# GpSimd issues the stores out of the staging buffers from the second block on, and the pacing bound of attention is 1.25 in place of 1.15

## The chip, the cores and the metric

One core of a Trainium2 chip runs the whole program. The metric is the device time of one execution in microseconds; the median of three timed executions is quoted, and a profiled execution stands beside it.

## What is computed

Three layers follow each other. The first is attention over 4 batches of 8 heads with 576 positions of 64 values: a coarse one on keys, queries and values averaged over 4 positions, and a local one for |i - j| < 4, added up.

```
out_d = softmax(scale * q_d k_d^T) v_d        # q_d, k_d, v_d: means of 4 positions
out_up = repeat(out_d, 4, axis=2)
out_local = softmax(where(|i - j| < 4, scale * q k^T, -1e9)) v
x = (out_up + out_local) as (2304, 512)
x = (sigmoid(x @ w_gate) * (x @ w_val)) @ w_out        # 512 x 1536, 512 x 1536, 1536 x 512
h = x @ w_in                                           # 512 x 2048
out = (h * tanh(softplus(h))) @ w_out2                 # 2048 x 512
```

The inputs are float64 in memory.

## The kernel before

**Precision and staging.** A weight tile is loaded by `load64` (L173, a DMA on SyncE, SP for short) as pairs of integers, and `narrow` makes floats of it: one ScalarE instruction (L180), three on VectorE (L182, L183, L187). `split` then makes two reduced-precision parts of every operand: the high part by a ScalarE cast (L192), the low one by a subtraction (L193) on VectorE. Each product is three TensorE matmuls: high by high, high by low, low by high.

**Blocks.** The program goes batch by batch, `block(b)`, b = 0 to 3, with 576 tokens each: `m1` (L977 to L979) makes gate and value, L982 and L983 combine them, and `fin` splits the product into G; `m1out` (L1008 to L1012) multiplies by w_out. While block b runs, the attention of block b + 1 is woven in by `weave`, and in blocks 1 and 2 also the weights of the second layer's output matrix, which are narrowed, split and written back to DRAM for later ("parked", `park_o2`, L1087). Block 1 runs from about 240 to 400 us, block 2 to 545, block 3 to 660; the second layer follows.

**The staging buffers.** There are two, handed out in turn by `stage_flat`. Both the results of `m1out` (ScalarE L1022 writes the high part, VectorE L1023 the low part, then the store L1028 to x2d) and the parked halves (cast L192, subtraction L193, store L1087 to wd2) go through them. Neither can be written again until the store that reads it has landed. There are 8 x 2 parked stores of 256 KB in block 1 and again in block 2, and 24 stores of 288 KB of results in blocks 1 to 3. All leave on SP's queue, among the loads of weights (L173, L221), of values (L332) and of tokens (L327).

**Attention.** Keys and queries are transposed (L418, L422) and averaged by GpSimd (`s_pool`, L447 and L449, into kd and qd), values by GpSimd too (`s_vpool`, L434 and L436, into vd; each asks SP for the next raw values at L332). The coarse scores are L510 into banks ps_g, with maximum L520 and L521 on VectorE and exponential L525 on ScalarE (Eg). The local part has scores L658, exponentials L680, transposes L723, copies of those by ScalarE (L97, ETl), and products L763 (ps_la); L782 adds the parts (xn), and xn is split for the next block. Attention has three PSUM banks, so a third score tile needs the exponential of an earlier one.

**What sets the order.** `weave` walks a clock of estimated costs and takes the next ready step of attention, weights or parking, or else the next piece of the block; a paced step is held back while its share of the work done is ahead of the block's own share by more than the bound of L932. The framework then schedules the instructions of each engine by a timeline of its own, so a change in who issues what can reorder all engines. Second-layer loads (L1149 of parked weights, L1153 of x2d) are issued by GpSimd in block 3 and after.

Of the kernel before, what the change touches and what calls it, by code (L numbers as in the profile page):

```python
# [8 lines left out]
F32 = mybir.dt.float32  # L9
# [39 lines left out]
def attn_moe_kernel(  # L49
# [13 lines left out]
    PE, DVE, ACT, POOL, SP = nc.tensor, nc.vector, nc.scalar, nc.gpsimd, nc.sync  # L63
# [22 lines left out]
    def subs(b):  # L86

        a = 2 * TQ if b == 0 else SUB
        return slice(0, a), slice(a, S)
# [34 lines left out]
    NU1 = KF1 + 2 * (KF1 // 4)  # L124
# [11 lines left out]
    def products():  # L136
        if not G:
            first.release()
            gpool = ctx.enter_context(tc.tile_pool(name="gpool", bufs=1, side="left", reuse_waits="tile"))
            G.append(gpool.tile([128, KF1 * 2 * S], F32R, name="G"))  # L140
        return G[0].rearrange("p (f z t) -> p f z t", f=KF1, z=2)
# [15 lines left out]
    def stage_flat():  # L157
        i = stage_n[0] % 2
        stage_n[0] += 1
        a = OS + i * 2 * SUBM  # L160
        return R[:, a:a + 2 * SUBM]

    def stage(n):
        return stage_flat()[:, 0:2 * n].rearrange("p (z t) -> p z t", z=2)
# [3 lines left out]
    x2d = dram.tile([128, 2, KD, NT], F32, name="x2d")  # L168
# [22 lines left out]
    def split(src, hi, lo, eng):  # L191
        ACT.copy(out=hi, in_=src)  # L192
        return eng.tensor_tensor(out=lo, in0=src, in1=hi.bitcast(F32), op=ALU.subtract)  # L193
# [711 lines left out]
    done_at = {}  # L905
# [3 lines left out]
    def weave(slots, steps):  # L909


        slots, steps = list(slots), list(steps)
        total_s = sum(z.cost for z in slots) or 1.0
        total_e = sum(z.cost for z in steps if z.paced) or 1.0
        at_s = at_e = 0.0

        def ready(z):
            t = 0.0
            for name, lat in z.deps:
                if name not in done_at:  # L920
                    return None
                t = max(t, done_at[name] + lat)
            return max([t] + bank_at[0:z.banks])

        while slots or steps:
            pick, soonest = None, None
            for z in steps:
                t = ready(z)
                if t is None:
                    continue  # L930
                if t <= clock[0]:
                    if z.cost and z.paced and slots and at_e / total_e > (ENG["PACE"] if ("slot", 0, NU1 - 1) not in done_at else 1.15) * at_s / total_s + 0.01:  # L932
                        continue
                    pick = z
                    break
                soonest = t if soonest is None else min(soonest, t)
            if pick is None and slots:
                t = ready(slots[0])
                if t is not None and t <= clock[0]:
                    pick = slots.pop(0)  # L940
                    at_s += pick.cost
                elif t is not None:
                    soonest = t if soonest is None else min(soonest, t)
            elif pick is not None:
                steps.remove(pick)
                if pick.paced:
                    at_e += pick.cost
            if pick is None:
                assert soonest is not None
                clock[0] = soonest  # L950
                continue
            pick.fn()
            clock[0] += pick.cost
            done_at[pick.name] = clock[0]
            for _ in range(pick.banks):
                bank_at.pop(0)
                bank_at.append(clock[0] + pick.hold)
# [4 lines left out]
    def flush():  # L962
        while late:
            late.pop(0)()
# [30 lines left out]
    def m1out(b, c2, fg, j, ps):  # L995
        hi, lo = wq[b, KF1 + c2 * (KF1 // 4) + fg]
        c, sub = divmod(j, 2)
        ts = subs(b)[sub]
        n = ts.stop - ts.start
        gt = products()  # L1000
        if fg == 0:
            ps[j] = mm.tile([128, 512], F32, tag="mm", name="ps_o")
        p = ps[j]
        last_g = KF1 // 4 - 1
        for i in range(4):
            f = 4 * fg + i
            o = i * 256 + c * 128
            PE.matmul(p[:, 0:n], lhsT=hi[:, o:o + 128], rhs=gt[:, f, 0, ts],  # L1008
                      start=(f == 0), stop=False)
            PE.matmul(p[:, 0:n], lhsT=hi[:, o:o + 128], rhs=gt[:, f, 1, ts],  # L1010
                      start=False, stop=False)
            PE.matmul(p[:, 0:n], lhsT=lo[:, o:o + 128], rhs=gt[:, f, 0, ts],  # L1012
                      start=False, stop=(f == KF1 - 1))
        flush()
        if fg == last_g:
            if b == B - 1 and c2:

                a = free_at[j // 2] + j % 2 * 1024
                t = R[:, a:a + 2 * n].rearrange("p (z t) -> p z t", z=2)
            else:  # L1020
                t = stage(n)
            ACT.activation(out=t[:, 0, :], in_=p[:, 0:n], func=AF.Copy, scale=0.5)  # L1022
            DVE.scalar_tensor_tensor(  # L1023
                out=t[:, 1, :], in0=p[:, 0:n], scalar=0.5, in1=t[:, 0, :].bitcast(F32),
                op0=ALU.mult, op1=ALU.subtract,
            )
            t0 = b * S + ts.start
            SP.dma_start(out=x2d[:, :, 2 * c2 + c, t0:t0 + n], in_=t.bitcast(F32))  # L1028

    def block(b, extra):  # L1030

        slots = []
        ps = {}

        def add(name, fn, cost, deps):
            slots.append(Step(name, fn, cost, [(d, 0.0) for d in deps]))

        pairs = [(f, sub) for f in range(KF1) for sub in range(2)]
        if b == 0:
            n = 2 * NRING  # L1040
            pairs = sorted(pairs[:n], key=lambda z: z[1]) + pairs[n:]
        for f, sub in pairs:
            deps = [("wp", b, f, 1)]
            deps += [(b, "split", i) for i, (q0, n) in enumerate(tiles) if q0 < subs(b)[sub].stop]
            add(("slot", b, f) if sub else ("half", b, f), lambda f=f, sub=sub: m1(b, f, sub), 10.25 * (subs(b)[sub].stop - subs(b)[sub].start), deps)

        def freed():
            flush()
            done_at[b + 1, "free"] = clock[0]

        add(("freed", b), freed, 0.0, [])
        for c2 in range(2):
            for fg in range(KF1 // 4):
                u = KF1 + c2 * (KF1 // 4) + fg
                for j in range(4):
                    add(("slot", b, u) if j == 3 else ("quarter", b, u, j),
                        lambda c2=c2, fg=fg, j=j: m1out(b, c2, fg, j, ps), 1475.0, [("wp", b, u, 1)])
        weave(slots, extra)
        flush()
# [22 lines left out]
    def park_o2(j, d):  # L1082
        for a in range(2):
            t = stage_flat()
            sl = slice(a * 256, (a + 1) * 256)
            split(d[:, sl], t[:, 0:256], t[:, 256:512], DVE)
            SP.dma_start(  # L1087
                out=wd2[j, :, :, sl], in_=t[:, 0:512].rearrange("p (z f) -> p z f", z=2).bitcast(F32)
            )

    if True:
# [3 lines left out]
        for z, offs in enumerate(((0, 3), (3, 3), (3, 0))):  # L1095
            for half, off in enumerate(offs):
                mv = mask[64 * half:64 * half + 64, z, :]
                POOL.affine_select(
                    out=mv, in_=mv, pattern=[[1, WK]], compare_op=ALU.is_ge, fill=-1e9 / scale,
# [3 lines left out]
                    out=mv, in_=mv, pattern=[[-1, WK]], compare_op=ALU.is_ge, fill=-1e9 / scale,  # L1103
# [4 lines left out]
        for b in range(B - 1):  # L1108
            extra = weights(b)
            if b == 0:  # L1110
                extra = attention(0) + extra
            extra += attention(b + 1)
            if b:
                srcs = [
                    (w2_out[j * 128:(j + 1) * 128, :].rearrange("(j p) f -> p j f", p=128), 1)
                    for j in range((b - 1) * per, b * per)
                ]
                extra += narrow_steps(
                    ("o2", b), srcs, clock[0] + 1000.0,
                    lambda i, d, b=b: park_o2((b - 1) * per + i, d), 9500.0,  # L1120
                )
            block(b, extra)
# [102 lines left out]
        for t in range(NT2):  # L1225
            if t > 0:
                po = [ops.tile([128, DM], F32, tag="o", name="po") for _ in range(2)]
            for gi in range(NG):
# [6 lines left out]
                n = 4 if t else 1  # L1235
# [50 lines left out]
```

## Time and profile before

| | us |
|---|---|
| median of three executions (1067.96 to 1068.79) | 1068.76 |
| profiled execution | 1070.58 |
| its span | 1068.8 |

The granted TensorE clock of the profiled execution was 0.987 of full speed on average. In the rows below, engines are PE (TensorE), DVE (VectorE), ACT (ScalarE), POOL (GpSimd) and SP (SyncE); a time in brackets at the end of a row is the idle time of the engine before it, with what ended it. R, G, d, wd, x2d and the like are the program's tile names; R<-d at L192 and L193 is a weight split, wd<-R a parked store.

### The profile page before, as it was taken

To read this page: it belongs to the slowest core of one execution; us is meant where nothing else is said; L and a number is where in the kernel's file an instruction comes from. 1 tells how busy PE (TensorE), PEld (TensorE's weight loads), DVE (VectorE), ACT (ScalarE), POOL (GpSimd) and SP (SyncE) were. 2 spreads that over 40 slices of the span, in tenths; PEclk is the share of its full clock that TensorE was granted. 3 is DMA by queue.
4 is the path that set the end of the run, shared out by engine and by line. 5 is a ranking of instruction groups with operands and counts; after the bars stand their busy time and mean duration, and the time that the engine had idled before them with its cause. 6 is when DMAs were issued, how large, how long until landed. Compare 5 with 4: busy or idle time off the path is not lost.

```text
span 1068.8 us, 20487 instructions
## 1 busy us (share of the span) xinstructions
PE 1005.6 (94%) x8152; PEld 941.9 (88%) x8152; DVE 688.9 (64%) x1129; ACT 520.4 (49%) x1222; POOL 193.3 (18%) x235
## 2 busy tenths in 40 slices
PE   4698988899989989999999999999999999999998
PEld 3587877799979989999999999999999999999997
DVE  6966988956976448965568951867555555555552
ACT  3644656455655447564546641654443443433432
POOL 5546574640300300300000002000000000000000
PEclk9989999999989999999999999999999999999999
DMA  7638666677762358632365658212112020220001
GB/s 171 195 87 220 178 200 218 199 231 245 226 196 74 104 168 254 203 133 80 105 202 183 205 179 267 61 25 59 24 37 60 1 59 4 57 59 1 21 1 40
DMA packets 122240, 134.51 MB, mean 126 GB/s; under 512 B 54432, under 2 KB 99488, under 8 KB 122144
## 3 DMA queue, kind: packets, MB, share of 16 engines
q1 hardware_dynamic: 110336, 115.37, 35.4%
q0 software_dynamic: 11808, 17.83, 6.3%
q8 instruction: 64, 1.05, 0.4%
q14 instruction: 32, 0.26, 0.1%
HBM read 101.19 MB, written 31.98 MB: 125 GB/s over the span
## 4 chain that ended last, share of the span: by engine, by line
PE 71%; DVE 11%; DMA 8%; ACT 4%; issue 3%; POOL 2%; SPq 0%; ACTq 0%; DVEq 0%; POOLq 0%
PE h L1180 6%; PE h L1182 6%; PE h L1181 6%; PE po L1190 6%; PE po L1188 6%; PE po L1189 6%; PE ps_m L977 6%; PE ps_m L978 6%; PE ps_m L979 6%; PE ps_o L1008 4%; PE ps_o L1012 4%; PE ps_o L1010 4%; DMA araw<-in_v_dram 2%; DVE d L183 2%; DMA raw<-in_moe_w_val_dram 2%
## 5 line engine op out<-in xcount | busy, mean ns | idle before, releaser
L977 PE MATMUL ps_m<-R 128*128 128x288 f32 (+2 forms) x768 | 234.1, 308 | 4.4 <-ACT R L192 3.0
L978 PE MATMUL ps_m<-R 128*128 128x288 f32 (+2 forms) x768 | 231.5, 302 | 2.1 <-POOL R L193 2.1
L979 PE MATMUL ps_m<-R 128*128 128x288 f32 (+2 forms) x768 | 231.0, 301 | 0.5 <-POOL R L193 0.5
L977 PEld LDWEIGHTS ps_m<-R 128*128 128x128 f32 x768 | 147.6, 193 | 9.1 <-ACT R L192 3.3
L978 PEld LDWEIGHTS ps_m<-R 128*128 128x128 f32 x768 | 148.1, 193 | 2.9 <-POOL R L193 2.2
L979 PEld LDWEIGHTS ps_m<-R 128*128 128x128 f32 x768 | 148.0, 193 | 1.4 <-POOL R L193 0.9
L192 ACT CAST R<-d 128x512 fp32r<-128x512 f32 (+1 forms) x192 | 108.7, 582 | 81.0 <-DVE d L187 38.7
L193 DVE TENSOR_TENSOR R<-d,R 128x512 fp32r<-128x512 f32 (+1 forms) x158 | 105.1, 679 | 43.1 <-ACT R L192 38.4
L1008 PE MATMUL ps_o<-G,R 128*128 128x288 f32 (+2 forms) x384 | 116.6, 304 | 0.0
L1012 PE MATMUL ps_o<-G,R 128*128 128x288 f32 (+2 forms) x384 | 114.5, 298 | 0.0
L1010 PE MATMUL ps_o<-G,R 128*128 128x288 f32 (+2 forms) x384 | 114.3, 298 | 0.0
L1188 PE MATMUL po<-R,G 128*128 128x512 f32 (+1 forms) x247 | 94.5, 383 | 0.0
L1189 PE MATMUL po<-R,G 128*128 128x512 f32 (+1 forms) x247 | 94.0, 381 | 0.0
L1190 PE MATMUL po<-R,G 128*128 128x512 f32 (+1 forms) x247 | 93.5, 383 | 0.0
L1201 ACT ACTIVATE e<-e 128x1024 f32<-128x1024 f32 (+1 forms) x48 | 40.6, 846 | 107.2 <-DVE e L1200 107.2
L1182 PE MATMUL h<-R 128*128 128x256 f32 x320 | 90.2, 282 | 0.0
L1181 PE MATMUL h<-R 128*128 128x256 f32 x320 | 90.2, 282 | 0.0
L1180 PE MATMUL h<-R 128*128 128x256 f32 x320 | 90.2, 282 | 0.0
L1200 DVE TENSOR_SCALAR e<-h 128x1024 f32<-128x1024 f32 (+1 forms) x48 | 45.9, 956 | 58.2 <-PE h L1182 58.0
L1008 PEld LDWEIGHTS ps_o<-G,R 128*128 128x128 f32 x384 | 73.3, 191 | 0.8
L180 ACT ACTIVATE rebias<-raw 128x512 f32<-128x512 f32 x68 | 45.9, 675 | 56.6 <-DMA raw<-in_moe_w_out_dram 23.2
L1010 PEld LDWEIGHTS ps_o<-G,R 128*128 128x128 f32 x384 | 73.2, 191 | 0.0
(137 smaller groups left out, 2258.3 us busy)
## 6 DMA issues: line engine op xcount, KB each, us to landing
d<-wd SPq DMA_DIRECT2D x54, 512.0 KB
raw<-in_moe_w_out_dram SPq DMA_DIRECT2D x28, 512.0 KB
wd<-d SPq DMA_DIRECT2D x18, 512.0 KB
wd<-R SPq DMA_DIRECT2D x32, 256.0 KB
raw<-in_moe_w_in_dram SPq DMA_DIRECT2D x16, 512.0 KB
x2d<-R SPq DMA_DIRECT2D x24, 288.0 KB
R<-wd POOLq DMA_DIRECT2D x13, 512.0 KB, 5.7
raw<-in_moe_w_gate_dram SPq DMA_DIRECT2D x12, 512.0 KB
```

The source lines that it names most:

```text
L977: PE.matmul(p[:, 0:n], lhsT=wh, rhs=xh[:, c, ts], start=(c == 0), stop=False)
L978: PE.matmul(p[:, 0:n], lhsT=wh, rhs=xl[:, c, ts], start=False, stop=False)
L979: PE.matmul(p[:, 0:n], lhsT=wl, rhs=xh[:, c, ts], start=False, stop=(c == KD - 1))
L1008: PE.matmul(p[:, 0:n], lhsT=hi[:, o:o + 128], rhs=gt[:, f, 0, ts], start=(f == 0), stop=False)
L1010: PE.matmul(p[:, 0:n], lhsT=hi[:, o:o + 128], rhs=gt[:, f, 1, ts], start=False, stop=False)
L1012: PE.matmul(p[:, 0:n], lhsT=lo[:, o:o + 128], rhs=gt[:, f, 0, ts], start=False, stop=(f == KF1 - 1))
L1180: PE.matmul(o, lhsT=wi[:, 0, c, cs], rhs=x[:, 0, c, :], start=(c == 0), stop=False)
L1181: PE.matmul(o, lhsT=wi[:, 0, c, cs], rhs=x[:, 1, c, :], start=False, stop=False)
L1182: PE.matmul(o, lhsT=wi[:, 1, c, cs], rhs=x[:, 0, c, :], start=False, stop=(c == KD - 1))
L1188: PE.matmul(p, lhsT=g[:, 0, ts], rhs=w[:, 0, cs], start=(j == 0), stop=False)
L1189: PE.matmul(p, lhsT=g[:, 0, ts], rhs=w[:, 1, cs], start=False, stop=False)
L1190: PE.matmul(p, lhsT=g[:, 1, ts], rhs=w[:, 0, cs], start=False, stop=(j == KF2 - 1))
```

## The change

Stores of results leave on GpSimd's queue in blocks 1 to 3 (block 0 stays on SP), parked stores leave on GpSimd's queue, and the bound by which attention may be ahead of a block's own work is 1.25 from block 1 on (block 0 has ENG["PACE"] as before, which is also 1.25).

```diff
--- before.py
+++ after.py
@@ -929,7 +929,7 @@
                 if t is None:
                     continue
                 if t <= clock[0]:
-                    if z.cost and z.paced and slots and at_e / total_e > (ENG["PACE"] if ("slot", 0, NU1 - 1) not in done_at else 1.15) * at_s / total_s + 0.01:
+                    if z.cost and z.paced and slots and at_e / total_e > (ENG["PACE"] if ("slot", 0, NU1 - 1) not in done_at else 1.25) * at_s / total_s + 0.01:
                         continue
                     pick = z
                     break
@@ -1025,7 +1025,7 @@
                 op0=ALU.mult, op1=ALU.subtract,
             )
             t0 = b * S + ts.start
-            SP.dma_start(out=x2d[:, :, 2 * c2 + c, t0:t0 + n], in_=t.bitcast(F32))
+            (POOL if b else SP).dma_start(out=x2d[:, :, 2 * c2 + c, t0:t0 + n], in_=t.bitcast(F32))
 
     def block(b, extra):
 
@@ -1084,7 +1084,7 @@
             t = stage_flat()
             sl = slice(a * 256, (a + 1) * 256)
             split(d[:, sl], t[:, 0:256], t[:, 256:512], DVE)
-            SP.dma_start(
+            POOL.dma_start(
                 out=wd2[j, :, :, sl], in_=t[:, 0:512].rearrange("p (z f) -> p z f", z=2).bitcast(F32)
             )
```

On GpSimd, around the pooling of keys (kd) and queries (qd) in block 1, there stood before:

```order
L193 TENSOR_TENSOR R_77<-d_2668,R_77 128x512 x2
L447 TENSOR_TENSOR kd_3440<-kT_2894 128x576
L449 TENSOR_TENSOR kd_3440<-kd_3440,kT_2894 128x576
L447 TENSOR_TENSOR qd_3497<-qT_2938 128x576
L449 TENSOR_TENSOR kd_3440<-kd_3440,kT_2894 128x576
L449 TENSOR_TENSOR qd_3497<-qd_3497,qT_2938 128x576 x2
L434 TENSOR_TENSOR vd_4808<-araw_4802 72x128
```

and now, with the parked stores (wd2):

```order
L1087 DMA wd2_82<-R_77 256x1x256 x8
L447 TENSOR_TENSOR kd_3440<-kT_2894 128x576
L1087 DMA wd2_82<-R_77 256x1x256
L449 TENSOR_TENSOR kd_3440<-kd_3440,kT_2894 128x576
L1087 DMA wd2_82<-R_77 256x1x256
L447 TENSOR_TENSOR qd_3497<-qT_2938 128x576
L449 TENSOR_TENSOR kd_3440<-kd_3440,kT_2894 128x576
L1087 DMA wd2_82<-R_77 256x1x256
L449 TENSOR_TENSOR qd_3497<-qd_3497,qT_2938 128x576
L1087 DMA wd2_82<-R_77 256x1x256
L449 TENSOR_TENSOR qd_3497<-qd_3497,qT_2938 128x576
```

All sixteen parked stores of the block now stand ahead of, between and behind the six pooling instructions.

On TensorE, around the second pair of coarse score tiles in block 1 (ps_g_3703 and ps_g_3704; ps_m are the block's own matmuls), the difference is:

```order
 L978 MATMUL ps_m_3683<-R_77 128x288
 L979 MATMUL ps_m_3683<-R_77 128x288
-L510 MATMUL ps_g_3703<-kd_3440,qd_3497 72x144
-L510 MATMUL ps_g_3704<-kd_3440,qd_3497 72x144
-L510 MATMUL ps_g_3703<-kd_3440,qd_3497 72x144
-L510 MATMUL ps_g_3704<-kd_3440,qd_3497 72x144
+L510 MATMUL ps_g_3703<-kd_3440,qd_3497 72x144 x2
 L977 MATMUL ps_m_3728<-R_77 128x288
 L978 MATMUL ps_m_3728<-R_77 128x288
```

and 20 matmuls further on:

```order
 L977 MATMUL ps_m_3741<-R_77 128x288
 L978 MATMUL ps_m_3741<-R_77 128x288
+L510 MATMUL ps_g_3704<-kd_3440,qd_3497 72x144 x2
 L979 MATMUL ps_m_3741<-R_77 128x288
 L977 MATMUL ps_m_3741<-R_77 128x288
```

The second tile of the pair moved behind 20 of the block's matmuls. The first pair (ps_g_3620, ps_g_3621) moved 23 of them later as well:

```order
 L977 MATMUL ps_m_3648<-R_77 128x288
 L978 MATMUL ps_m_3648<-R_77 128x288
+L510 MATMUL ps_g_3620<-kd_3440,qd_3497 72x144
+L510 MATMUL ps_g_3621<-kd_3440,qd_3497 72x144
+L510 MATMUL ps_g_3620<-kd_3440,qd_3497 72x144
+L510 MATMUL ps_g_3621<-kd_3440,qd_3497 72x144
 L979 MATMUL ps_m_3648<-R_77 128x288
 L977 MATMUL ps_m_3670<-R_77 128x288
```

It stood between ps_m_3596 and ps_m_3635 before.

On ScalarE, ahead of the exponentials of the first pair (Eg_3618), there stood before:

```order
L192 CAST G_951<-sg_3609 128x288
L192 CAST R_77<-d2_4027 128x256 x2
L192 CAST R_77<-d_3668 128x512
L982 ACTIVATE sg_3661<-ps_m_3635 128x288
L525 ACTIVATE Eg_3618,sum_3617<-ps_g_3620,m_3616 72x144 x2
L525 ACTIVATE Eg_3618,sum_3617<-ps_g_3621,m_3616 72x144 x2
```

and now:

```order
L180 ACTIVATE rebias_4885<-raw_4806 128x512
L192 CAST R_77<-d2_4027 128x256 x2
L192 CAST G_951<-sg_3661 128x288
L982 ACTIVATE sg_3696<-ps_m_3670 128x288
L180 ACTIVATE rebias_5109<-raw_4974 128x512
L525 ACTIVATE Eg_3618,sum_3617<-ps_g_3620,m_3616 72x144 x2
L525 ACTIVATE Eg_3618,sum_3617<-ps_g_3621,m_3616 72x144 x2
```

The conversion of the next raw weights (L180, rebias_5109) and one more cast of G come ahead of the exponentials, and one cast of d_3668 stands earlier.

At the end of block 1 GpSimd had only its value adds (vd); now the first result stores (x2d) stand among them:

```order
L436 TENSOR_TENSOR vd_4808<-vd_4808,araw_4877 72x128
L436 TENSOR_TENSOR vd_4808<-vd_4808,araw_4942 72x128
L436 TENSOR_TENSOR vd_4808<-vd_4808,araw_4877 72x128
L1028 DMA x2d_83<-R_77 256x1x288
L436 TENSOR_TENSOR vd_4808<-vd_4808,araw_4942 72x128
L1028 DMA x2d_83<-R_77 256x1x288
L434 TENSOR_TENSOR vd_4808<-araw_5020 72x128
L436 TENSOR_TENSOR vd_4808<-vd_4808,araw_5020 72x128
```

On SP the loads of raw values (araw) and the result stores stood in turn before:

```order
L332 DMA araw_4877<-in_v_dram 72x2x256
L332 DMA araw_4942<-in_v_dram 72x2x256
L221 DMA d_4792<-wd_81 128x1024
L1028 DMA x2d_83<-R_77 256x1x288
L332 DMA araw_5020<-in_v_dram 72x2x256
L332 DMA araw_5072<-in_v_dram 72x2x256
L1028 DMA x2d_83<-R_77 256x1x288
L221 DMA d_4794<-wd_81 128x1024
L1028 DMA x2d_83<-R_77 256x1x288 x2
```

The stores left this queue. On ScalarE, the staging casts (L1022, out of ps_o) and the copies of local attention (ETl) stood there before as:

```order
L192 CAST R_77<-d_4296 128x512 x2
L1022 ACTIVATE R_77<-ps_o_4238 128x288
L1022 ACTIVATE R_77<-ps_o_4255 128x288
L97 COPY ETl_4517<-ps_lt_4512 128x512
L97 COPY ETl_4575<-ps_lt_4570 128x512
```

and now:

```order
L192 CAST R_77<-d_4296 128x512 x2
L1022 ACTIVATE R_77<-ps_o_4238 128x288
L97 COPY ETl_4517<-ps_lt_4512 128x512
L1022 ACTIVATE R_77<-ps_o_4255 128x288
L97 COPY ETl_4575<-ps_lt_4570 128x512
```

The first copy moved ahead of the fourth staging cast. At the step into block 2 ScalarE had:

```order
L192 CAST G_951<-sg_4860 128x288
L192 CAST R_77<-d2_4884 128x256
L422 COPY kT_4821<-ps_t_4822 128x4x128
L192 CAST R_77<-d2_4884 128x256
L192 CAST R_77<-xn_2864 128x4x112
L422 COPY qT_4865<-ps_t_4866 128x4x128
```

and now has:

```order
L192 CAST G_951<-sg_4860 128x288
L192 CAST R_77<-d2_4884 128x256
L422 COPY kT_4821<-ps_t_4822 128x4x128
L192 CAST R_77<-xn_2864 128x4x112
L422 COPY qT_4865<-ps_t_4866 128x4x128
L192 CAST R_77<-d2_4884 128x256
```

The cast of xn moved ahead of the second cast of d2_4884.

## Rows read from the trace of the kernel before

**Rows 1.** The page, busy time, share of the span and instructions of each engine

```profile
PE 1005.6 (94%) x8152; PEld 941.9 (88%) x8152; DVE 688.9 (64%) x1129; ACT 520.4 (49%) x1222; POOL 193.3 (18%) x235
```

**Rows 2.** Windows: us, busy time and instructions of each engine, PEclk, DMA share, GB/s

```profile
300.00:320.00 20.00, 15.83 (x103) 14.68 (x102) 14.83 (x36) 11.21 (x36) 0.00 (x0) 0.83 0.52 167
360.00:380.00 20.00, 16.01 (x170) 15.45 (x170) 9.04 (x22) 9.88 (x42) 9.19 (x18) 0.96 0.51 156
560.00:660.00 100.00, 100.00 (x758) 100.00 (x757) 65.60 (x130) 47.34 (x101) 7.35 (x13) 1.00 0.61 197
```

**Rows 3.** Waits of TensorE from 242 us on: total us, times, longest us

```profile
PE ps_g L510 <- ACT Eg L525: 5.0, 2, 4.2
PE ps_la L763 <- ACT ETl L97: 4.0, 1, 4.0
PE ps_m L977 <- ACT R L192: 3.0, 2, 2.3
PE ps_m L977 <- DVE sg L983: 1.3, 1, 1.3
PE ps_t L418 <- DVE xn L782: 0.8, 1, 0.8
```

**Rows 4.** Line L510 in 290:320 (ns min/median/max, first and last start us); TensorE's timeline (start, us)

```profile
L510 PE MATMUL ps_g<-kd,qd x24: 282/283/510, 295.5 to 317.9; 64*72 64x144 f32 x24
...
307.81 1.23 PE L510 MATMUL ps_g<-kd,qd 64*72 64x144 f32 x6 [4.17 <-ACT Eg L525]
```

**Rows 5.** Windows after the idle time at 303.6 us, columns as in group 2

```profile
309.00:313.00 4.00, 4.00 (x18) 4.00 (x18) 2.77 (x7) 2.19 (x6) 0.00 (x0) 0.50 0.77 254
314.00:318.00 4.00, 4.00 (x36) 3.79 (x34) 3.07 (x6) 2.83 (x11) 0.00 (x0) 1.00 0.01 2
```

**Rows 6.** The chain of waits through that idle time: start us, us, what

```profile
294.92 4.38 DMA wd<-R
...
299.75 0.43 DVE R L193
...
300.21 5.52 DMA wd<-R
```

**Rows 7.** ScalarE's timeline there: start us, us, instruction [idle before <-releaser]

```profile
299.63 0.43 ACT L192 CAST G<-sg 128x288 fp32r<-128x288 f32 x1
...
300.58 0.67 ACT L180 ACTIVATE rebias<-raw 128x512 f32<-128x512 f32 x1 [0.22 <-DMA raw<-in_moe_w_out_dram]
...
305.80 0.92 ACT L192 CAST R<-d 128x256 fp32r<-128x256 f32 x2 [2.74 <-DMA wd<-R]
```

**Rows 8.** Timelines of GpSimd (first row) and VectorE around the pooling

```profile
289.17 4.06 POOL L449 TENSOR_TENSOR qd<-qd,qT 128x576 f32<-128x576 f32 x2
...
289.45 2.19 DVE L193 TENSOR_TENSOR R<-d,R 128x512 fp32r<-128x512 f32 x1
...
298.86 0.68 DVE L193 TENSOR_TENSOR R<-d,R 128x512 fp32r<-128x512 f32 x1
```

**Rows 9.** SP's timeline, a parked store

```profile
293.54 0.52 SPq L1087 DMA_DIRECT2D wd<-R  x1
```

**Rows 10.** End of block 1: SP's timeline, the chain of waits (two rows), ScalarE's timeline

```profile
366.62 0.56 SPq L1028 DMA_DIRECT2D x2d<-R  x1
...
370.82 2.14 POOL vd L436 x4
...
373.34 3.44 DMA x2d<-R
...
376.88 0.41 ACT L1022 ACTIVATE R<-ps_o 128x288 fp32r<-128x288 f32 x1 [4.39 <-DMA x2d<-R]
```

**Rows 11.** GpSimd's DMA lines L1153, L1149: issue ns min/median/max; landing of L1149

```profile
L1153 POOL DMA_DIRECT2D R<-x2d x10: 740/747/936, 546.8 to 952.1; - x10
...
L1149 POOL DMA_DIRECT2D R<-wd x13: 528/536/558, 548.5 to 669.1; - x13
...
DMA to landing us min/median/max: 3.7/5.9/9.0
```

## The prediction

> **What bounds the kernel now.** I read the page's list of engines first: TensorE is busy for 94% of the span [rows 1], so a change elsewhere counts only where it moves an idle time of TensorE. The windows say where such idle time is. The change touches nothing in block 0, so I look from 242 us on: between 300 and 320 us TensorE works 15.83 of 20 us, between 360 and 380 us 16.01, while from 560 to 660 us it never stops [rows 2]. The waits of TensorE name the idle times [rows 3]: 5.0 us for a global score (L510) behind the exponential at L525, 4.0 us for L763 behind the ScalarE copy at L97, 3.0 us for L977 behind a ScalarE cast, 1.3 behind VectorE at L983 and 0.8 for L418. Together 14.1 us.
>
> I call the places A (block 1, 303.6 to 307.8 us: 4.17 of the 5.0 us) [rows 4], B (end of block 1, the 4.0 us), C (step from block 1 to 2: 0.8 us of L418 and 0.7 of L977), D (block 2: 1.3 us of L977 and the remaining 0.8 of L510) and E (block 2 to 3: the remaining 2.3 us of L977). A costs more than its idle time: from 309 to 313 us the granted clock was 0.50, the 1.2 GHz level, and 18 matmuls ran where 36 run in the 4 us from 314 on [rows 5]. That is 2.0 us. So the ceiling for any gain is 14.1 us and what the low clock adds, 2.0 us behind A and, as an upper estimate, as much behind B and E: 20 us.
>
> **A, priced.** The chain of waits through A is made of two stores out of the two staging buffers, 4.38 and 5.52 us from issue to landing [rows 6]. A parked half needs a free buffer, its cast on ScalarE waits for the store before it (305.80, 2.74 us idle) [rows 7], and L525 stands behind the casts in ScalarE's order. The store's issue on SP is no part of that wait: VectorE's subtraction ends at 299.75 + 0.43 = 300.18 us and the store is issued at 300.21 [rows 6]. So issuing from GpSimd takes nothing off this chain. It was put so late by an earlier delay: while GpSimd pools keys and queries, VectorE's two-input subtractions take 2.19 us where one takes 0.68 alone [rows 8].
>
> What does move is the order. In the changed program TensorE does the second two products of the second score pair 20 matmuls later. At 36 matmuls in 4 us [rows 5] that is 20 x 0.111 = 2.2 us that used to come after the stall. One product more (0.28 us) [rows 4] goes ahead too. Against it, on ScalarE L180 (0.67 us) and a 288-wide cast (0.43) come ahead of L525, and one 512-wide weight cast, 0.92 less 0.43 = 0.5 us, leaves [rows 7]: +0.6 us, if the raw load that L180 reads has landed. GpSimd's issue of a store I price by its loads: 0.54 us (L1149) to 0.75 us (L1153) [rows 11], against 0.52 on SP [rows 9], so at most 0.23 us more for each of the two stores of the chain; I take 0.2 for both. The stall becomes 4.17 - 2.2 - 0.3 + 0.6 + 0.2 = 2.5 us: **-1.7 us** for A. I leave the low clock as it is. Bounds: were the stall and its low clock gone, -4.2 - 2.0 = -6.2; were all that is saved eaten by later stores, up to +2 (below).
>
> **The move past GpSimd's other work.** In block 1 eight of the parked weights' stores stand ahead of the pooling's six instructions on GpSimd and four between them (in block 2 nine and four), and the last pooling add of block 1 stands behind the twelfth store, which left SP at 293.54 us [rows 9]. Adding 0.65 us of issue and one add (4.06 us for two, so 2.03) [rows 8] it ends at 296.3 us, 3.0 us later than the 293.2 us of before. The first score group, which needs it, is moved back 23 matmuls, 2.6 us, from its 295.5 us [rows 4] to 298.1 us. So this is hidden with 1.8 us to spare: 0, but it is the thinnest cover in the change. VectorE may even lose less beside spread adds; I don't count that.
>
> **B.** Before, the first store of the block's results that matters here leaves SP at 366.62 us; the next one leaves at 373.34, behind the loads that wait for GpSimd's value adds (370.82 to 372.96), and lands 3.44 us later, at 376.8 [rows 10]. ScalarE's fourth staging cast (376.88) waited 4.39 us for it, and L97, for which TensorE waits, comes behind that cast. In the changed order the first store itself stands behind the third of those adds, at about 370.82 + 3/4 x 2.14 = 372.4 us. But L97 now stands ahead of the fourth staging cast, so it waits for the landing of that first store alone: 372.4 + 0.2 of longer issue + 3.44 to 5.52 (both seen in this trace [rows 6, 10]) = 376.0 to 378.1 us, against 376.8. That is -0.8 to +1.3, and I take the middle, **+0.3 us**; the store's pieces are more like those of L1153, whose issue took up to 0.94 us [rows 11], so the upper end stays in the range.
>
> **C and D.** At C the cast of xn moves ahead of a 256-wide weight cast (under the 0.43 us of 288 columns [rows 7]): **-0.3 us** of the 0.7. At D the split of the score pair is made again, with 13 or more matmuls between, 1.4 us, which covers the 0.8 us; the 1.3 us behind L983 may grow by a store issue between the pooling adds: -0.8 + 0.3 = **-0.5 us**, with +-2 for stores that wait behind pooling adds of 2 us [rows 8].
>
> **The rest at nothing.** E's chain doesn't pass a store. Block 3's stores move behind GpSimd's loads for the second layer, and TensorE never idles there [rows 2]; the loads that follow are for work some tens of us later. 56 stores at 0.65 us are 36 us of issue on GpSimd, which is busy for 18% of the span [rows 1]. The new pace constant lets attention steps through earlier; a step that it lets through displaces matmuls of the same length on a full TensorE, so by itself 0.
>
> **Sum:** -1.7 + 0.3 - 0.3 - 0.5 = -2.2 us. The profiled execution took 1070.6 us (its span 1068.8), so 1068.4 of that kind; the median of the timed runs lies 1.8 us lower, at 1068.76, and I lay the sum on it: 1066.6 us.
>
> **A rule against the change.** No issue of a weight load on GpSimd took longer than 0.558 us [rows 11], though VectorE was busy for 66 of the 100 us in which most of them lie [rows 2]. The Trainium skill (SBUF — State Buffer, section "SBUF: two separate sides") says that descriptors of a GpSimd-issued DMA are written by GpSimd and wait while VectorE holds the port pair the two share in its fast copy modes. By that rule it is the landing that comes late rather than the issue, which the issue times can't rule out; what it would give is rival 4.
>
> **Rivals.**
> 1. *The larger gain.* Stores on their own queue no longer stand behind the 512 KB loads on SP's queue, and land nearer the 3.44 us than the 5.52. Two landings 2.1 us shorter take A's remaining 2.5 us away and its low clock, and 1 us of B: -2.2 - 2.5 - 2.0 - 1.0 = -7.7 us, 1061.1 us. For it: the two stores of A run while the DMA engines are full. Against: the same engines carry both.
> 2. *The stores don't matter.* The wait moves from one place of the chain to the next: A's 2.2 us return at the third score pair, since L525 still comes at the same time. 1068.8 us.
> 3. *Slower: stores and pooling hold each other up on GpSimd* (blocks 1 and 2). Each pooling step there stands behind a store that needs a free staging buffer, and so an earlier landing. If four of these are each 1.1 us later (5.52 against 4.38), the last add comes 4.4 us later, past its spare 1.8: 2.6 us of new idle time, and 2.0 of low clock, and A's gain goes: +4.6 + 1.7 - 2.2 = +4.1 us, 1072.9 us. It decides once the pooling ends later than 298.1 us. For it: GpSimd works in order. Against: the spare time.
> 4. *Slower: descriptors wait for VectorE.* The longest landing of a GpSimd load was 9.0 us, 3.1 over the median [rows 11]. If each store pays that, A's two stores cost 6.2 us and B's one 3.1: -2.2 + 9.3 = +7.1 us, 1075.9 us. The page named above makes this its rule.
>
> **How the numbers follow.** A measurement of this kernel can tell 0.2%, 2.1 us, from no change. My forecast, a small gain of 0.5 to 4.5 us, has 0.45, of which just over half (0.25) lies beyond 2.1 us; rival 1 has 0.17, rival 2 0.14, rival 3 0.17, rival 4 0.07. Faster: 0.25 + 0.17 = 0.42. Same: 0.20 of the forecast + 0.14 + 0.01 of rival 3 = 0.35. Slower: 0.16 + 0.07 = 0.23. The forecast's own range is 1064.3 to 1068.3 us. The range for 8 in 10 reaches from 1060.5 to 1073.5 us: it leaves out a third of rival 1 (0.06), some 0.07 of rival 3, and rival 4 (0.07).
>
> **What would show it.** Right: TensorE's wait for L525 in block 1 at 2 to 3 us instead of 4.17; the first score group without a wait; the wait at L763 at 3.5 to 5; GpSimd's issue of L1087 and L1028 at 0.5 to 0.95 us. Wrong: TensorE waiting for kd or qd of the pooling (rival 3); stores that land 3 us later than from SP (rival 4), or at 3 us in A (rival 1); a wait at the third score pair as large as the one saved (rival 2); a new idle time in block 3.

## The result, and the profile after

| | before | after |
|---|---|---|
| median of six executions, us | 1068.55 | 1076.53 |
| lowest to highest, us | 1065.97 to 1071.68 | 1073.59 to 1078.96 |
| profiled execution and its span, us | 1070.58, 1068.8 | 1076.76, 1075.0 |

The ratio is 1.0070, 95% interval 1.0046 to 1.0094: the change made the kernel 0.7% slower, about 7.5 us. The prediction was 1066.6 us, with 1060.5 to 1073.5 for 8 in 10; the median lies beyond its upper end and on the other side of the kernel before.

First the page's list of engines after (busy us, share of the span, instructions):

```profile
PE 1011.9 (94%) x8152; PEld 947.1 (88%) x8152; DVE 691.1 (64%) x1129; ACT 520.9 (48%) x1222; POOL 231.5 (22%) x291
```

Then windows of the same execution (us, busy time and instructions of PE, PEld, DVE, ACT and POOL, granted clock, DMA share, GB/s):

```profile
300.00:320.00 20.00, 16.05 (x104) 14.38 (x105) 15.84 (x36) 11.55 (x36) 2.81 (x5) 0.91 0.64 211
360.00:380.00 20.00, 16.97 (x183) 16.45 (x182) 8.60 (x19) 9.33 (x41) 10.91 (x21) 1.00 0.41 127
440.00:460.00 20.00, 17.93 (x133) 16.70 (x131) 18.15 (x28) 8.10 (x20) 8.82 (x9) 1.00 0.55 170
460.00:480.00 20.00, 16.77 (x107) 15.68 (x107) 12.23 (x28) 12.08 (x43) 0.69 (x1) 0.83 0.35 108
560.00:660.00 100.00, 99.47 (x746) 98.72 (x745) 66.75 (x131) 48.80 (x104) 8.60 (x14) 1.00 0.61 195
```

Beside [rows 1], TensorE is *busy* 6.3 us longer, in a span that is 6.2 us longer, with the same matmuls: a part of the loss stands in the granted clock. (That the idle time is 63 us in either span comes from block 0: with the same code it had 3 us less of it in this execution, more of the low clock, and took 1.6 us longer.) Beside [rows 2], the stretch of 300 to 320 us has 16.05 us of work in place of 15.83, and 360 to 380 us 16.97 in place of 16.01; 560 to 660 us is still nearly full. What is new is 460 to 480 us, in block 2: 16.77 us of work at a granted clock of 0.83.

How long each block took says it more plainly. I take the end of the last w_out matmul (L1008 to L1012) of each block from TensorE's timeline, and the differences:

| block, us | 1 | 2 | 3 | from there to the end |
|---|---|---|---|---|
| before | 150.0 | 142.6 | 119.6 | 410.1 |
| after | 147.0 | 150.3 | 119.5 | 410.2 |

Block 1 gained 3.0 us, block 2 lost 7.7. From windows of 2 us, TensorE's idle time and what the clock was short of full speed, added up: in block 1, 8.6 and 5.1 us before, 7.4 and 1.7 after; in block 2, 3.6 and 0.0 us before, 7.5 and 3.4 after. So block 2 lost about as much idle time as clock, and block 1's gain is mostly clock. Blocks 1 and 2 together lost 4.7 us in this pair of executions, not the whole 7.5 us of the medians; another 1.6 us is block 0, whose code is the same. Because of it block 1 began at 248.1 us, 246.4 before, and block 2 at 395.1 us, 396.5 before, so below I also count lateness from the start of a block. Now the waits of TensorE from 242 us on (total us, times, longest us):

```profile
PE ps_g L510 <- ACT Eg L525: 7.1, 2, 3.9
PE ps_m L977 <- ACT R L192: 3.2, 2, 2.2
PE ps_la L763 <- ACT ETl L97: 3.0, 1, 3.0
PE ps_g L510 <- POOL qd L449: 1.4, 2, 0.9
PE ps_m L977 <- DVE sg L983: 1.3, 2, 1.2
PE ps_t L418 <- DVE xn L782: 1.2, 1, 1.2
```

Against [rows 3], L763 (the place B of the prediction) fell from 4.0 to 3.0 us. L510 behind L525 rose from 5.0 to 7.1 us: 3.9 of it in block 1, where it had been 4.17, and 3.2 in block 2, where it had been 0.8. And there is a wait that did not exist, for the pooled queries, 1.4 us.

### The profile page after: what moved, and what is told of

Same layout as the page of the kernel before. It is cut to its first block, busy times and chain, and to the rows that moved or that the text cites. A ratio compares the mean times of both kernels' runs of the same rounds, so it can differ in the third digit from the quotient of the medians.

```text
span 1075.0 us, 20484 instructions
## 1 busy us (share of the span) xinstructions
PE 1011.9 (94%) x8152; PEld 947.1 (88%) x8152; DVE 691.1 (64%) x1129; ACT 520.9 (48%) x1222; POOL 231.5 (22%) x291
## 4 chain that ended last, share of the span: by engine, by line
PE 68%; DVE 13%; DMA 9%; issue 5%; ACT 4%; POOL 2%; SPq 0%; ACTq 0%; DVEq 0%; POOLq 0%
PE h L1180 6%; PE h L1182 6%; PE h L1181 6%; PE po L1190 6%; PE po L1188 6%; PE po L1189 6%; PE ps_m L977 5%; PE ps_m L978 5%; PE ps_m L979 5%; PE ps_o L1008 4%; PE ps_o L1010 3%; PE ps_o L1012 3%; DVE d L183 2%; DVE d L182 2%; DMA raw<-in_moe_w_in_dram 2%
## 5 line engine op out<-in xcount | busy, mean ns | idle before, releaser
L977 PE MATMUL ps_m<-R 128*128 128x288 f32 (+2 forms) x768 | 235.1, 309 | 5.9 <-ACT R L192 4.2
L977 PEld LDWEIGHTS ps_m<-R 128*128 128x128 f32 x768 | 148.7, 195 | 10.9 <-ACT R L192 4.7
L1008 PE MATMUL ps_o<-G,R 128*128 128x288 f32 (+2 forms) x384 | 115.9, 302 | 0.0
L1012 PE MATMUL ps_o<-G,R 128*128 128x288 f32 (+2 forms) x384 | 113.8, 297 | 0.0
L180 ACT ACTIVATE rebias<-raw 128x512 f32<-128x512 f32 x68 | 45.9, 676 | 61.4 <-DMA raw<-in_moe_w_in_dram 22.6
L1008 PEld LDWEIGHTS ps_o<-G,R 128*128 128x128 f32 x384 | 72.6, 189 | 0.8
L1012 PEld LDWEIGHTS ps_o<-G,R 128*128 128x128 f32 x384 | 72.7, 189 | 0.1
```

Of the source, the lines that this page charges most:

```text
L977: PE.matmul(p[:, 0:n], lhsT=wh, rhs=xh[:, c, ts], start=(c == 0), stop=False)
```

## Where the time went

The pooled queries come late. On GpSimd's timeline after, the last two adds of block 1, each behind a parked store (start, us, [idle before, releaser]):

```profile
293.61 0.68 POOL L1087 DMA_DIRECT2D wd<-R  x1 [4.23 <-DVE R L193]
294.22 1.84 POOL L449 TENSOR_TENSOR qd<-qd,qT 128x576 f32<-128x576 f32 x1
297.62 0.68 POOL L1087 DMA_DIRECT2D wd<-R  x1 [1.56 <-DVE R L193]
298.24 1.80 POOL L449 TENSOR_TENSOR qd<-qd,qT 128x576 f32<-128x576 f32 x1
```

And the last two of block 2:

```profile
444.18 0.68 POOL L1087 DMA_DIRECT2D wd<-R  x1 [1.56 <-DVE R L193]
444.80 1.79 POOL L449 TENSOR_TENSOR qd<-qd,qT 128x576 f32<-128x576 f32 x1
451.30 0.68 POOL L1087 DMA_DIRECT2D wd<-R  x1 [4.70 <-DVE R L193]
451.91 1.80 POOL L449 TENSOR_TENSOR qd<-qd,qT 128x576 f32<-128x576 f32 x1
```

The store L1087 waits on GpSimd for VectorE's subtraction (4.23 and 1.56 us in block 1, 1.56 and 4.70 us in block 2), and the add behind it waits too, though its own operands have long been there. The pooling ends at 298.24 + 1.80 = 300.0 us in block 1, not at 293.2 [rows 8], and at 451.91 + 1.80 = 453.7 us in block 2. Counted from the start of the block it ends after 52.0 us (46.8 before) and after 58.7 us (48.6 before). Before, block 2's last two adds were one row of GpSimd's timeline, and they ended at 445.1 us:

```profile
441.06 4.03 POOL L449 TENSOR_TENSOR qd<-qd,qT 128x576 f32<-128x576 f32 x2
```

Meanwhile VectorE is held up as it was before, by whichever add runs then: one of its rows in block 1 and three in block 2 after, where alone the first two take 0.45, the third 0.68 and the fourth 0.42 us.

```profile
294.18 2.21 DVE L193 TENSOR_TENSOR G<-sg,G 128x288 fp32r<-128x288 f32 x1 [0.50 <-ACT G L192]
...
434.37 2.48 DVE L193 TENSOR_TENSOR G<-sg,G 128x288 fp32r<-128x288 f32 x1
...
440.49 2.70 DVE L193 TENSOR_TENSOR R<-d,R 128x512 fp32r<-128x512 f32 x1
...
444.41 2.47 DVE L182 TENSOR_SCALAR d<-rebias 128x512 int32<-128x512 int32 x1
```

Before and after, every instruction of VectorE that took over 0.3 us longer than the median of its kind in these two blocks overlapped an add on GpSimd. So each side waits for the other: the add for the store, the store for a subtraction on VectorE, and that subtraction is late because an instruction ahead of it in VectorE's order is long while another add runs. In block 2 the late first scores then met a second delay. The chain of waits through the new idle time (start us, us, what):

```profile
455.59 4.84 DMA raw<-in_moe_w_in_dram
...
461.02 0.42 ACT G L192
...
461.84 0.42 DVE R L193
462.37 0.83 ACT Eg L525 x4
463.25 1.23 PE ps_g L510 x4
```

And the ScalarE instruction that waits for the load at the chain's head, from ScalarE's timeline:

```profile
460.45 0.66 ACT L180 ACTIVATE rebias<-raw 128x512 f32<-128x512 f32 x1 [2.42 <-DMA raw<-in_moe_w_in_dram]
```

ScalarE's order has the conversion of the next raw weights (L180) ahead of a cast of G; VectorE's subtraction for that cast stands ahead of the maximum's last step, and the exponential L525 needs that. The raw load was issued at 455.59 us and landed 4.84 us later; ScalarE stood idle 2.42 us for it, and the first scores waited. TensorE waited 3.23 us, and then ran at the 1.2 GHz level, 0.50 of the full clock, as a window shows (columns as above):

```profile
464.00:468.50 4.50, 4.50 (x19) 4.13 (x19) 2.73 (x7) 2.33 (x6) 0.00 (x0) 0.50 0.56 158
```

In these 4.5 us it did 19 matmuls, at half the pace of the second window of [rows 5]: 2.2 us more.

Issue and landing of the parked stores from GpSimd explain little of this. Line L1087 after (issue in ns, min/median/max; then from issue to landing):

```profile
L1087 POOL DMA_DIRECT2D wd<-R x32: 680/687/917, 251.6 to 462.6; - x32
...
DMA to landing us min/median/max: 2.5/3.7/7.1
```

0.69 us of issue, near the 0.65 of the prediction, and a median landing of 3.7 us; the two of SP's stores that the chain before shows took 4.4 and 5.5 us [rows 6]. The longest landing, 7.1 us, was that of the eighth store of block 1, issued at 277.19 us; ScalarE waited 1.49 us for it.

## The experiments

My theory from the two traces: **the pooling of keys and queries and the parked stores hold each other up on GpSimd, so the pooled tiles come late, and that costs.** Its rivals: the pace; the result stores, or every store on GpSimd by itself (issue, landing). Each run below is timed against runs of the kernel before on its chip; the ratio and its 95% interval are given, and then the lengths of blocks 1 and 2 by the measure above, from the one profiled execution (before: 150.0 and 142.6 us).

**One part at a time.** The pace alone, `e1_pace`:

```diff
- ... else 1.15) * at_s / total_s + 0.01
+ ... else 1.25) * at_s / total_s + 0.01
```

> Only the pacing bound is 1.25, all stores stay on SP. Theory (the loss is made on GpSimd, where the two pooled tiles kd and qd wait between parked stores): 0, within 2 us of the kernel before, since GpSimd's order and the places of the coarse scores are those of before. Rival (the pace lets attention and the conversions run too early and is the cause): 5 to 8 us slower, with the wait of L510 in block 2 at 3 us as in the changed kernel.

0.9982 (0.9965 to 0.9998), blocks of 147.8 and 141.5 us. The pace did not cost; it even gave back 0.2%, just clear of no change, which the prediction had as 0.

The result stores alone, `e2_x2d`:

```diff
-            SP.dma_start(out=x2d[...
+            (POOL if b else SP).dma_start(out=x2d[...
```

> Only the 24 result stores (L1028) of blocks 1 to 3 move to GpSimd; the parked stores and the pace stay. Theory: between 2 us faster and 1 us slower than before; the wait at L763 shrinks from 4.0 to about 3 us as in the changed kernel, the pooling ends at about 293 and 445 us as before. Rival (a store from GpSimd costs by itself, by its issue or its landing): 2 to 4 us slower.

1.0026 (1.0005 to 1.0046): slower by 0.3%, outside what the theory expected. Blocks of 148.6 and 145.9 us: block 1 shorter as expected, block 2 3.3 us longer. Its waits of TensorE in blocks 1 and 2:

```profile
PE ps_g L510 <- ACT Eg L525: 5.7, 2, 3.9
PE ps_la L763 <- ACT ETl L97: 2.9, 1, 2.9
```

L763 fell to 2.9 us as expected. L510 did not, though no store stands among the adds here (1.8 us of its 5.7 are in block 2, 0.8 before). By what way block 2 got longer here I did not find out.

The parked stores alone, `e3_park`:

```diff
-            SP.dma_start(
+            POOL.dma_start(
                 out=wd2[j, :, :, sl], ...
```

> Only the 32 parked stores (L1087) move to GpSimd; result stores and pace stay. Theory: the whole loss, 5 to 9 us slower than before; pooling in block 2 ends near 453 us in place of 445 us and TensorE waits about 3 us at L510 there. Rival (it is the result stores, or only both together with the pace): within 2 us of before.

1.0112 (1.0086 to 1.0138): 12 us slower, more than the 5 to 9 expected and more than the whole change. Blocks of 153.5 and 148.4 us. The wait that the theory named:

```profile
PE ps_g L510 <- ACT Eg L525: 6.5, 2, 3.4
```

3.4 of it in block 2, as expected about 3. The last pooling add ended at 456.3 us, in an execution that came to block 2 some 5 us later. So most of the loss is the parked stores'. That the whole change lost less is not clear of noise (its interval ends at 1.0094), and the next run, without the pace, lost as much as the whole change, so the pace is not shown to take a part back. Both kinds of store without the pace, `e5_pool` (the two store edits above):

> Both kinds of store on GpSimd, the pace stays 1.15 (the changed kernel without its pace). Theory: GpSimd's order is that of the parked stores alone, so the loss is between that of the parked stores alone (12 us) and that of the changed kernel (8 us): 8 to 13 us slower than before. Rival (only all three parts together make the loss): within 3 us of before.

1.0074 (1.0049 to 1.01), blocks of 149.0 and 150.1 us: at the lower edge of the expected, the size of the whole change. There the conversion that stands ahead of the first exponential in block 1 of the changed kernel stands behind it, and TensorE still waited 3.45 us for that exponential; so the stall in block 1 does not need that place in the order.

**Only the stores among the adds.** `e4_mid_sp` is the changed kernel with the stores of steps 4 to 6 on SP:

```diff
-            POOL.dma_start(
+            (SP if j % per in (4, 5, 6) else POOL).dma_start(
                 out=wd2[j, :, :, sl], ...
```

> The changed kernel, but the six parked stores of steps 4 to 6 in each block leave on SP again, so that no store stands between the pooling's instructions on GpSimd; 20 parked stores and all result stores stay on GpSimd, the pace stays 1.25. Theory: the loss is gone, within 2 us of before, or up to 2 us faster. Rival (each store on GpSimd costs, whatever its place): two thirds of the loss stay, 4 to 5 us slower than before.

1.0008 (0.9988 to 1.0029): the loss against the kernel before is gone, with 20 of 32 parked stores and all result stores still on GpSimd. The pace's own gain is in this: against `e1_pace`, on the same chip and with the same pace, it is 2.5 us slower (medians of twelve, 1068.18 and 1065.66), about what `e2_x2d` lost. So the stores outside the pooling may cost 2 to 3 us. The last two adds of block 1 in one row of GpSimd's timeline:

```profile
286.70 4.30 POOL L449 TENSOR_TENSOR qd<-qd,qT 128x576 f32<-128x576 f32 x2
```

And two waits of TensorE in blocks 1 and 2:

```profile
PE ps_m L977 <- DVE sg L983: 4.6, 2, 3.3
...
PE ps_g L510 <- ACT Eg L525: 2.3, 1, 2.3
```

The pooling ends at 291.0 us, and L510 waits 2.3 us in all, 5.0 before. Block 1 took 145.6 us, 4.4 less than before; block 2 took 146.4 us, with a wait of 3.3 us behind VectorE's L983, held up beside the adds. So the place of six stores in each block decides about most of the loss of the change, and block 2's loss is not wholly made by it.

**Late, without a store in the way.** `e6_late` is the kernel before with four more GpSimd instructions behind the queries' pooling in blocks 1 and 2, multiplications by 1:

```diff
                 for r in range(2, FAC):
                     eng.tensor_tensor(out=t, in0=t, in1=src[:, :, :, r], op=ALU.add)
+                if b > 1 and nm == "q":
+                    for _ in range(4):
+                        eng.tensor_scalar(out=t, in0=t, scalar1=1.0, scalar2=None, op0=ALU.mult)
```

> The kernel before, all stores on SP, with four multiplications of the pooled queries by 1 on GpSimd behind the pooling in blocks 1 and 2, so that the pooled queries come some 4 to 8 us later without any store in the way. Theory (lateness of the pooled tiles is what costs): 4 to 10 us slower than before, with TensorE waiting at L510 or at its exponential in both blocks. Rival (lateness costs nothing, since the first coarse scores have room; what costs is the stores that wait in GpSimd's queue): within 2 us of before.

1.0077 (1.0053 to 1.0101), blocks of 153.1 and 148.4 us. The row of the added instructions in block 2 on GpSimd's timeline:

```profile
445.69 7.89 POOL L452 TENSOR_SCALAR qd<-qd 128x576 f32<-128x576 f32 x4
```

And the wait of TensorE at the coarse scores (L513 here, for three lines more):

```profile
PE ps_g L513 <- ACT Eg L528: 4.7, 2, 2.5
```

The queries of block 2 are ready at 453.6 us, 56.9 us from the start of the block (58.7 in the changed kernel, 48.6 before), and the cost is of the same size, with every store on SP. But it is not a clean measure, in three ways. VectorE's instructions were lengthened by more, 10.4 us in block 1 and 9.5 in block 2 against 8.7 and 8.0 before (each instruction less the median of its line, tiles and shape, where longer, from 240 to 400 and from 400 to 545 us). The wait that the theory named did not grow in both blocks: it was 2.5 us in block 1, 4.17 before, and 2.2 us in block 2, 0.8 before; in each block TensorE waited 1.7 to 1.8 us behind VectorE's L983 (L986 here) as well, 1.3 us in block 2 alone before. And TensorE's order changed too. The first coarse scores of block 2 stand in one row, long after the queries were ready:

```profile
460.75 1.20 PE L513 MATMUL ps_g<-kd,qd 64*72 64x144 f32 x12
```

The order goes with the lateness in all the runs. In the kernel before, in e1, e2, e4 and in all the runs further down, the first coarse scores stand behind 312 of a block's 576 matmuls of gate and value, and they come in eights; in the changed kernel, e3 and e5 they stand behind 335 to 339, with the next ones split in fours; here behind 376 or 377. The framework lays that order by its own timeline before anything runs. So the runs show that stores (or other work) among the adds cost; they do not part the late arrival itself from the order that the framework made for it.

**No pooling on GpSimd.** If stores and adds hold each other up, taking the adds away must free the stores. `e7_dvepool` is the changed kernel with this, `e8_pace_dvepool` the pace alone with this, `e9_dve_only` the kernel before with this and nothing else:

```diff
-                add(("pool", nm), s_pool(nm, POOL if b > 1 else DVE), ...
+                add(("pool", nm), s_pool(nm, DVE), ...
```

> The changed kernel with the pooling of keys and queries on VectorE in blocks 1 and 2 too; all stores of blocks 1 to 3 stay on GpSimd, whose queue then holds no pooling. Theory (stores and pooling hold each other up): the loss goes, within 3 us of before, or faster, since VectorE no longer works beside GpSimd's adds. Rival (the place of the stores on GpSimd costs through issue or landing): 4 to 8 us slower, as the changed kernel.

> The pacing bound 1.25, the pooling on VectorE in blocks 1 and 2, all stores on SP. A try at a faster kernel: if VectorE loses more beside GpSimd's adds (about 7 us in either block) than the six adds cost it (about 7 us by the halves in block 0), 1 to 3 us faster than before; if VectorE's added work delays the casts behind the stall in block 1, 1 to 3 us slower.

> The kernel before with the pooling of keys and queries on VectorE in blocks 1 and 2, stores on SP, pace 1.15: neither part of the change. Theory (the pooling on GpSimd is what made the stalls in the middle of blocks 1 and 2, and the stores on GpSimd only lengthened it): 8 to 12 us faster than before, as with the pace or with all of the change. Rival (the gain of the earlier run needs the stores on GpSimd or the pace): within 4 us of before.

> The changed kernel with pooling on VectorE once more, beside the version without the change on the same chip. If the change is worth something once no pooling stands in GpSimd's queue, it is 1 to 3 us below e9_dve_only; theory says about the same, within 2 us, since no stall of blocks 1 and 2 then passes a store of the parked weights.

| | ratio to before | 95% interval | block 1, us | block 2, us |
|---|---|---|---|---|
| e7, all of the change | 0.9891 | 0.9868 to 0.9914 | 139.0 | 141.0 |
| e10, the same kernel again | 0.9904 | 0.9875 to 0.9933 | 141.6 | 142.2 |
| e8, the pace alone | 0.9903 | 0.9875 to 0.9930 | 139.8 | 142.1 |
| e9, none of the change | 0.9907 | 0.9876 to 0.9938 | 142.9 | 139.7 |

All four are about 1% faster than before, some 10 us, and they can't be told apart. For e7 I had expected no loss, for e8 1 to 3 us; that it would gain 10 I had not. e9, forecast after them at 8 to 12 us, gained 9.8. e9 and e10 ran on the same chip: with no pooling in GpSimd's queue the 56 stores there (and the pace) make no difference that can be told, -0.4 us between the medians. So a price for each store cannot be the 7.5 us of the change, though 2 to 3 us, as e2 and e4 have them, lie within the intervals. The rival that the gain needs the change falls. In `e9_dve_only`, the waits of TensorE in blocks 1 and 2:

```profile
PE ps_la L763 <- ACT ETl L97: 3.5, 1, 3.5
PE ps_m L977 <- ACT R L192: 2.9, 2, 2.3
PE ps_t L418 <- DVE xn L782: 0.8, 1, 0.8
```

Two of its windows:

```profile
300.00:320.00 20.00, 20.00 (x164) 19.26 (x163) 15.53 (x36) 14.65 (x50) 0.00 (x0) 1.00 0.54 179
460.00:480.00 20.00, 20.00 (x211) 19.32 (x211) 12.65 (x29) 12.50 (x39) 0.00 (x0) 1.00 0.26 82
```

And two rows of its VectorE timeline in block 1, a subtraction and a pooling add:

```profile
277.74 0.68 DVE L193 TENSOR_TENSOR R<-d,R 128x512 fp32r<-128x512 f32 x1
...
282.16 1.20 DVE L449 TENSOR_TENSOR kd<-kd,kT 128x576 f32<-128x576 f32 x1
```

L510 is not in the list of waits any more, and the two stretches are full: both stalls at the coarse scores are gone. An add of L449 takes VectorE 1.20 us where GpSimd took 1.8 to 2.2, the subtraction beside it takes its 0.68 us again, and what VectorE loses by lengthened instructions falls from 8.7 to 0.7 us in block 1 and from 8.0 to 0.8 in block 2. Six adds of 1.2 us are 7.2 us of new work for VectorE, yet its busy time fell from 97.3 to 95.1 us in block 1 and from 97.4 to 95.8 in block 2: it does the pooling in less time than it lost beside it.

Last, the value adds off GpSimd as well, `e11_dvepool_vd` (in `s_vpool`, of e7):

```diff
-                eng = eng_[ENG["vd.%d" % n]] if b == 0 else POOL
+                eng = eng_[ENG["vd.%d" % n]] if b == 0 else DVE
```

> The changed kernel with the pooling and the value adds (L434, L436) on VectorE too, so that GpSimd's queue in blocks 1 to 3 holds DMAs alone. Theory: the wait at L763, at the end of block 1, where the first result store stood behind value adds, goes from 2.8 us to under 1.5, and the time is 1 to 3 us below e10. Rival (the landing of the stores sets that wait): L763 stays at 2.5 to 4 us and the time within 1.5 us of e10.

0.9900 (0.9870 to 0.9929), blocks of 140.0 and 140.1 us; against e10 on the same chip no difference. The wait at L763:

```profile
PE ps_la L763 <- ACT ETl L97: 2.2, 1, 2.2
```

2.2 us against 2.6 in e10 and 2.8 in e7, which is the same kernel as e10: less than the theory's fall to under 1.5, and below the rival's 2.5 to 4. The value adds held the first result store up for a small part of the wait at most. The landing rather than GpSimd's queue is likely to set what is left, but that is only argued.

## Why the prediction was wrong, point by point

- **The bound.** Right: TensorE's few idle times in blocks 1 to 3 and the low clock behind them were what was won or lost, and block 3 and the second layer did not move (119.5 and 410.2 us).
- **A, -1.7 us.** The idle time came out at 3.86 us and 0.50 us for the pooled queries, so 4.4 against 4.17; predicted 2.5. The order did move as read, but L525 came later by more than TensorE did: the queries were late and the raw load too. Its low clock, left as it is in the sum, fell from 3.4 to 1.7 us. Nor is 4.17 us a firm base: with the scores in their old order the same wait was 2.45 us in e1, 3.9 in e2 and 2.29 in e4. The prediction's own condition, "if the raw load that L180 reads has landed", did not hold; ScalarE waited twice for one (1.94 and 0.69 us):

```profile
306.52 0.68 ACT L180 ACTIVATE rebias<-raw 128x512 f32<-128x512 f32 x1 [1.94 <-DMA raw<-in_moe_w_out_dram]
...
310.21 0.68 ACT L180 ACTIVATE rebias<-raw 128x512 f32<-128x512 f32 x1 [0.69 <-DMA raw<-in_moe_w_out_dram]
```

- **The move past GpSimd's other work, 0.** This is the step that failed, in two ways. First, it took the store at 293.54 us [rows 9] for the twelfth of the block. SP's timeline before has ten parked stores of block 1 ahead of it, so it is the eleventh; the twelfth is the next:

```profile
294.92 0.52 SPq L1087 DMA_DIRECT2D wd<-R  x1
```

One add stands behind the eleventh and one behind the twelfth. By the prediction's own rule the first ends at 293.54 + 0.65 + 2.03 = 296.2 us and the second at 296.2 + 0.65 + 2.03 = 298.9 us, 0.8 us past the mark of 298.1: the 1.8 us to spare were not there. Second, the time at which a store leaves is not given from outside: it waits for a subtraction that the adds hold up. In block 1 that was 1.56 us at the twelfth store (297.62 us), and the last add ended at 300.0; counted from the start of the block that is 0.3 us past the mark, and TensorE waited 0.50 us for it. In block 2 the last store among the adds left at 451.30 us, 447.67 before, and the queries came 8.6 us late (10.0 from the start of the block). What the prediction put at 0 is 1.4 us of waits for the queries, and behind them the late exponentials of A and D.
- **B, +0.3 us.** The wait fell by 1.0 us, just past the lower bound of -0.8 to +1.3, and the low clock behind it went too (0.96 in 360 to 380 us before, 1.00 after), which the sum had not counted. The order of the copies did this, as read; the middle of the bounds was too high, since the store landed at the short end of the times seen.
- **C and D, -0.3 and -0.5 us.** C came out 0.7 us worse (L418 1.2 and L977 1.0). D was the mis-sized term: block 2 lost 7.7 us, of which D's waits are 3.2, 0.9 and 1.2 us against 0.8 and 1.3 before, and 3.4 us are clock. The split of the score pair, which should have covered the wait, was not enough, since the queries came 8.6 us late and the raw load landed late behind them. I had worked the pooling's end out for block 1 and taken block 2 to be like it, with +-2 us.
- **The pace, 0**, gave 0.2% (e1). **The stores' price**, 0.65 us of issue, was 0.69; rival 4, descriptors that wait for VectorE, priced 3.1 us more for each landing and did not happen in this kernel: no issue of L1087 took over 0.92 us and the median landing was 3.7 us. The wait of descriptors that the Trainium skill describes (SBUF — State Buffer, section "SBUF: two separate sides") did not show here.
- **Rival 3** was what happened, mutual waiting of stores and adds, with 0.17, and the sign that was set for it, TensorE waiting for the pooled queries, came. Its price, 1072.9 us, was too low: it put the idle time into block 1, and the larger part came in block 2. Its weight was too small because I set against it a spare time that came of the miscounted store and of its old time.
- **Rival 1's reason** may have been there: parked stores landed in 3.7 us at the median, the two of the old chain in 4.4 and 5.5. It gave no gain: in A and D TensorE now waited behind the late queries and a raw load.

The Trainium skill (DMA: Bandwidth & Descriptors, section "Issuing engines are not separate DMA queues") says that starting DMAs from several engines saves no more than the time on the sequencer that starts them. e9 and e10 agree: 0.9907 and 0.9904 with the stores on SP or on GpSimd. What a waiting DMA does to the compute that stands behind it in the same engine's order comes on top, and that made most of the cost here.

## What to carry to other kernels

A DMA that waits for another engine's result is an instruction in its issuing engine's order: put on an engine with compute of its own, everything behind it waits too. An engine's idle share does not show that; ask for each piece of compute which wait stands ahead of it, count off that it is the right one, and move the times of those waits with the change instead of keeping them from the old trace. And where two engines lengthen each other's instructions, try the work on one of them: here VectorE did the adds in less time than it had lost beside them, and that was worth 1%, more than anything that the change was about.

## What I had not expected of the hardware

- VectorE's instruction with one input in memory (L182) was lengthened beside GpSimd's adds as well: 2.47 us in the row at 444.41 above, 0.42 alone.
- A store from GpSimd landed in 3.7 us at the median (L1087, 2.5 to 7.1), no later than the two from SP that the chain before showed, 4.4 and 5.5 us.
